# Attention with top-32 masks and two expert layers: one more pipeline step, and for 20 tiles the mask is applied on TensorE

## The chip, the cores and the metric

The kernel runs on one core of a Trainium2 chip. The metric is the device time of one execution in microseconds (us). The engines are TensorE (PE, its weight loads PEld), VectorE (DVE), ScalarE (ACT), GpSimd (POOL) and SyncE (SP), which issues DMAs. Each runs its own queue in order.

## The reference

```python
# q, k, v: (4, 8, 576, 64); top_k = 32
scores = scale * q @ k.T                       # per batch and head, 576 x 576
kth = np.partition(scores, -32)[..., -32:-31]  # 32nd largest of each row
scores = np.where(scores >= kth, scores, -1e9)
attn = softmax(scores); x = attn @ v           # (2304 tokens, 512)
h = x @ w_in                                   # 512 -> 2048
x = (h * clip(h + 3, 0, 6) / 6) @ w_out        # 2048 -> 512
# then: each token goes to one of 8 experts (argmax of x @ w_gate):
out = gate_w * (relu(x @ w1[e]) @ w2[e])       # 512 -> 1024 -> 512
```

## The kernel before

**Tiles.** Attention runs over 144 tiles, each 128 query rows of one head against 576 keys. For a tile t, PE makes the scores (`qk`, in fp32r with the queries split in a high and a low part), ACT copies them out of PSUM (`sevac`, line 300 by way of `copy`), DVE takes the largest values of eight pieces of 72 columns (line 660) and from these the 24 largest (lines 666, 671). The 24th largest, a little lowered, is the value u (`top_c`). The 32nd largest is then found among the scores at or below u: `z` holds the scores with all above u removed, line 731 takes its eight largest, `act_sign` counts on ACT how many scores are above u, and `match` (line 735) picks the one with the right rank as threshold `tall`. `act_exp` makes exp(score - max) on ACT, and `mask` (line 739, DVE, 128x576) sets to zero what is below the threshold. `trans` transposes the masked tile on PE in chunks of 128 columns into the PSUM tile `ptps`, `tevac` copies it out on ACT, `pv` multiplies it with the values, `xevac` divides by the sum, `xt` transposes into the x buffers of the first expert layer.

**The first 20 tiles (`ZPE`).** Their z isn't made on DVE: POOL makes `zw`, -2^100 where the score is above u and 0 elsewhere, in bf16 (`z_pe`, line 703), and PE adds it to a second computation of the scores in the PSUM tile `yps2` (`qk(t, zw)`, line 630). That PSUM tile is used by the first expert layer from about tile 22 on, so later tiles make z on DVE (line 696).

**The layer.** Blocks of 256 tokens are 16 tiles of attention. When all tiles of a block are through `xt`, 16 steps of the first expert layer (`moe_step`: `l1`, line 863; `epi_a`, 869; `epi_b`, 875; `epi_c`; `l2`, line 894) run for it, one for each tile step. Its weights come in 64 bits and are converted on the way, 32 pieces in some 34 tile steps (`conv64`: ACT lines 328, 333; DVE lines 329, 336, 339; POOL lines 298, 347). After the last attention tile the rest of the layer's steps follow, and then the 8 experts (lines 1263, 1286).

**Order.** One loop over tile steps traces all this; each operation gets a priority, 400 a step plus an offset of its kind (`PRIO`), and a scheduler orders each engine's queue by priority among what is ready in its own model. So work of later steps can stand earlier in a queue.

```python
for t in range(T + 7):
    trans(t - 4); top_c(t - 1); act_exp(t - 1)
    qk(t + LA); pv(t - 5); sevac(t + LA); xevac(t - 5)      # LA = 2
    tevac(t - 4); act_sign(t - 1)
    top_a(t, [moe_step, mask(t - 2), conv_next, ...])       # interleaved
    top_z(t - 1); z_pe(t - 1)
```

Of the kernel before, what the change touches and what calls it, by code (L numbers as in the profile page):

```python
# [26 lines left out]

HUGE = 2.0 ** 100
AGE = 0
KB = 1  # L30
LA = 2
# [26 lines left out]
def attention_two_moe_kernel(  # L58
# [169 lines left out]
    def body(cs, exact, ends=None):  # L228
# [160 lines left out]
        if not exact:  # L389
            identb.append(ap1.tile([P, P], BF16, name="identb"))  # L390
            G.tensor_copy(identb[0], ident)
        NPB, NSB, VB = 3, 3 + LA, 2

# [304 lines left out]
        def z_pe(t):  # L698
            if exact or not 0 <= t < ZPE:
                return  # L700
            pr("zw")
            zw = ap1.tile([P, S], F32, tag="z", bufs=2, name=f"z{t}").bitcast(BF16)[:, 0:S]
            G.tensor_scalar(zw, ts[t]["s"][:, 0:S], ts[t]["u"], -HUGE, op0=ALU.is_gt, op1=ALU.mult)
            qk(t, zw)

# [8 lines left out]
        def act_sign(t):  # L714
            if exact:
                return
            pr("sign")
            d = ts[t]
            jk = ap1.tile([P, S], BF16, tag="jk", bufs=1, name=f"jk{t}")
            d["sg"] = ap1.tile([P, 1], F32, tag="sg", bufs=3, name=f"sg{t}")  # L720
            A.activation(jk, d["s"][:, 0:S], AF.Sign, bias=ts[t]["u"], scale=-1.0, accum_out=d["sg"])  # L721

        def mask(t):
            if not 0 <= t < T:
                return
            d = ts[t]
            if not exact:
                pr("max8")
                z8 = ap1.tile([P, 8], F32, tag="z8", bufs=3, name=f"z8_{t}")
                j8 = ap1.tile([P, 8, 2], F32, tag="j8", bufs=1, name=f"j8_{t}")  # L730
                V.max(z8, d["z"])  # L731
                A.activation(zall[:, t:t + 1], z8[:, 1:2], AF.Sign, bias=ts[t]["u"], scale=-1.0)
                yield
                pr("match")
# [11 lines left out]
            yield  # L746


        def trans(t):
            pr("trans")  # L750
# [3 lines left out]
            for c in range(NFC):  # L754
                PE.transpose(ptps[:, c * P:(c + 1) * P], pb[:, c0 + c * P:c0 + (c + 1) * P], ident)  # L755
            if o == "T" or o[0]:
                PE.transpose(ptps[:, N4:SW], pb[:, N4:SW], ident)  # L757

        def tevac(t):
            pr("tevac")  # L760
            d = ts[t]
            o = tiles[t][1]
            if o == "T" or o[0]:
                d["pt"] = ap1.tile([P, SW], F32, tag="ptb", bufs=PTB, name=f"pt{t}")
                copy(mod(t, TPOOL), d["pt"], ptps[:, 0:SW])
            else:
                d["pt"] = ap1.tile([P, N4], F32, tag="pta", bufs=PTA, name=f"pt{t}")
                copy(mod(t, TPOOL), d["pt"], ptps[:, 0:N4])

# [331 lines left out]
        cacc = 0  # L1101
        for t in range(T + 7):
            pr0[0] = pbase + t * STEP
            loads(t)
            if t == 5:
                load_gates(ts[5]["s"])
            while vloaded[0] < NV and (vloaded[0] < VB or vlast[vloaded[0] - VB] <= t - 6):
                load_v()
            ms = moe_step()
            next(ms, None)  # L1110
            if 0 <= t - 4 < T:
                trans(t - 4)
# [6 lines left out]
            if 0 <= t - 5 < T:  # L1119
                pv(t - 5)  # L1120
            if t + LA < T:
                sevac(t + LA)
            if 0 <= t - 5 < T:
                xevac(t - 5)
            xg = None
            if xtq and (xtq[0][2] < t - 5 or t >= T):
                xg = xt(*xtq.pop(0))
                next(xg)
            if 0 <= t - 4 < T:
                tevac(t - 4)  # L1130
            if xg:
# [10 lines left out]
            cacc += CRATE  # L1142
            others = [ms, mask(t - 2)]
            while cacc >= 16:
# [14 lines left out]
        if not exact:  # L1159
            fl = ap1.tile([P, S], F32, tag="z", bufs=2, name="fl")[:, 0:T]  # L1160
            V.tensor_scalar(fl, zall, 0.0, None, op0=ALU.is_le)
            V.scalar_tensor_tensor(fl, uall, HUGE, fl, op0=ALU.is_ge, op1=ALU.add)
            V.scalar_tensor_tensor(fl, tall, 0.0, fl, op0=ALU.is_le, op1=ALU.add, accum_out=flag[:, 0:1])
        pr0[0] += STEP
# [295 lines left out]
```

## Time and profile before

| what | value |
|---|---|
| median of 3 runs | 1199.18 us (1198.66 to 1202.45) |
| profiled execution | 1204.39 us, span 1202.5 us |
| busy in the span | PE 93%, PEld 83%, DVE 78%, ACT 67%, POOL 38% |
| mean granted clock of TensorE | 0.961 of full |
| chain that ended last | PE 71%, DVE 16%, issue 5%, ACT 4% |

Busy time is the time in which an engine has an instruction at work; a matmul's end is modelled, so PE busy is not PE at its peak. Idle time of an engine that isn't the limit costs nothing. The stages differ: PE is below 80% busy up to about 150 us and above 95% later.

### The profile page before, as it was taken

To read this page: it belongs to the slowest core of one execution; us is meant where nothing else is said; L and a number is where in the kernel's file an instruction comes from. 1 tells how busy PE (TensorE), PEld (TensorE's weight loads), DVE (VectorE), ACT (ScalarE), POOL (GpSimd) and SP (SyncE) were. 2 spreads that over 40 slices of the span, in tenths; PEclk is the share of its full clock that TensorE was granted. 3 is DMA by queue.
4 is the path that set the end of the run, shared out by engine and by line. 5 is a ranking of instruction groups with operands and counts; after the bars stand their busy time and mean duration, and the time that the engine had idled before them with its cause. 6 is when DMAs were issued, how large, how long until landed. Compare 5 with 4: busy or idle time off the path is not lost.

```text
span 1202.5 us, 24061 instructions
## 1 busy us (share of the span) xinstructions
PE 1118.5 (93%) x7414; PEld 1003.8 (83%) x7414; DVE 940.9 (78%) x3853; ACT 807.6 (67%) x2082; POOL 458.5 (38%) x668
## 2 busy tenths in 40 slices
PE   5677688999999999999999999999999899999995
PEld 4566577778999989999988899999888799888885
DVE  5989989999999999998999899999641554545540
ACT  4777877778878788778778788777541353444441
POOL 5877646644332354433342432322344311222110
PEclk9668879999999999999999999999999899999998
DMA  3654456564553555754444554543486555455530
GB/s 76 189 179 142 143 171 221 162 174 125 157 134 113 151 134 142 177 135 135 118 122 126 133 147 125 152 133 110 127 271 163 176 187 179 161 176 185 160 121 31
DMA packets 184123, 179.24 MB, mean 149 GB/s; under 512 B 123629, under 2 KB 148509, under 8 KB 183984
## 3 DMA queue, kind: packets, MB, share of 16 engines
q1 hardware_dynamic: 178960, 167.24, 48.3%
q0 software_dynamic: 3872, 10.08, 2.6%
q8 instruction: 61, 1.00, 0.4%
q14 instruction: 78, 0.64, 0.2%
q10 hardware_dynamic: 1152, 0.28, 0.1%
HBM read 159.53 MB, written 18.61 MB: 148 GB/s over the span
## 4 chain that ended last, share of the span: by engine, by line
PE 71%; DVE 16%; issue 5%; ACT 4%; POOL 2%; DMA 2%; SPq 0%; POOLq 0%; ACTq 0%; DVEq 0%
PE l1ps L863 15%; PE yps L894 13%; PE ptps L789 9%; PE lp L1263 8%; PE ops L1286 8%; PE sps L630 6%; PE ptps L755 4%; DVE cd L660 2%; DVE pbuf L739 2%; DVE z L696 2%; DVE z L731 1%; PE ptps L935 1%; DVE m L666 1%; DVE cw L671 1%; PE misc L474 1%
## 5 line engine op out<-in xcount | busy, mean ns | idle before, releaser
L894 PE MATMUL yps<-wo,gh 128*128 128x512 f32 x544 | 206.7, 418 | 0.1
L298 POOL TENSOR_SCALAR gh<-gf 128x256 fp32r<-128x256 f32 x144 | 72.7, 505 | 345.2 <-PE yps L894 196.0
L660 DVE MAX8 cd<-sbuf 128x8 f32<-128x72 f32 x1152 | 187.9, 218 | 3.4 <-ACT sbuf L300 3.2
L863 PE MATMUL l1ps<-xh,wih 128*128 128x256 f32 x576 | 167.6, 291 | 4.7 <-DVE gf L875 3.1
L863 PE MATMUL l1ps<-xh,wil 128*128 128x256 f32 x576 | 164.0, 285 | 0.0
L863 PE MATMUL l1ps<-xl,wih 128*128 128x256 f32 x576 | 163.9, 285 | 0.0
L789 PE MATMUL ptps<-vn,pt 128*128 128x65 f32 (+1 forms) x1152 | 145.8, 281 | 0.0
L789 PEld LDWEIGHTS ptps<-vn,pt 128*128 128x128 f32 x1152 | 143.0, 201 | 0.0
L739 DVE SCALAR_TENSOR_TENSOR pbuf<-sbuf,tall,pbuf 128x576 f32<-128x576 f32 x144 | 136.8, 950 | 0.1
L883 POOL TENSOR_TENSOR gl<-gf,gh 128x256 fp32r<-128x256 f32 x144 | 125.5, 871 | 11.4
L863 PEld LDWEIGHTS l1ps<-xh,wih 128*128 128x128 f32 x576 | 110.4, 192 | 14.9 <-DVE gf L875 7.6
L1036 DVE TENSOR_TENSOR wl<-raw,wh 128x1024 fp32r<-128x1024 f32 x64 | 78.6, 1236 | 53.7 <-ACT wh L1035 51.6
L721 ACT ACTIVATE jk<-sbuf,uall 128x576 bf16<-128x576 f32 x144 | 111.6, 775 | 4.2 <-DVE j L735 0.9
L863 PEld LDWEIGHTS l1ps<-xl,wih 128*128 128x128 f32 x576 | 110.6, 192 | 4.2
L712 ACT ACTIVATE pbuf<-sbuf,nb 128x576 f32<-128x576 f32 x144 | 111.2, 775 | 4.1 <-PE ptps L757 0.9
L894 PEld LDWEIGHTS yps<-wo,gh 128*128 128x128 f32 x544 | 101.2, 190 | 14.8 <-POOL qh L486 0.3
L300 ACT ACTIVATE sbuf<-sps 128x576 f32<-128x576 f32 x144 | 92.9, 645 | 30.4 <-PE sps L630 16.5
L869 ACT ACTIVATE gf<-l1ps,three 128x256 f32<-128x256 f32 x144 | 67.9, 471 | 66.9 <-PE l1ps L863 55.7
L755 PE MATMUL ptps<-ident,pbuf 128*128 128x128 f32 x576 | 93.9, 286 | 19.7 <-DVE j L735 12.6
L894 PE MATMUL yps<-wo,gl 128*128 128x512 f32 x272 | 110.4, 406 | 0.6 <-POOL gl L883 0.6
L863 PEld LDWEIGHTS l1ps<-xh,wil 128*128 128x128 f32 x576 | 110.6, 192 | 0.1
L630 PE MATMUL sps<-kx,qh 128*128 128x288 f32 (+2 forms) x336 | 96.8, 319 | 14.3 <-ACT sbuf L300 10.5
(259 smaller groups left out, 2974.7 us busy)
## 6 DMA issues: line engine op xcount, KB each, us to landing
wo<-wod SPq DMA_DIRECT2D x144, 512.0 KB, 3.8
raw<-in_moe_w_dram SPq DMA_DIRECT2D x64, 512.0 KB, 4.3
vn<-in_v_dram SPq DMA_DIRECT2D x96, 128.0 KB, 2.7
rawi<-in_moe_w_in_dram SPq DMA_DIRECT2D x16, 512.0 KB, 4.0
rawo<-in_moe_w_out_dram SPq DMA_DIRECT2D x16, 512.0 KB, 4.6
wod<-wc SPq DMA_DIRECT2D x16, 512.0 KB, 5.6
qn<-in_q_dram SPq DMA_DIRECT2D x126, 64.0 KB, 2.5
yd<-y SPq DMA_DIRECT2D x18, 258.0 KB, 5.1
```

The lines of the kernel that those rows point to most:

```text
L630: PE.matmul(d_, a_, b_, start=(i == 0), stop=(i == len(mm) - 1))
L660: V.max(cd[:, c, :], s[:, c * CK:(c + 1) * CK])
L712: A.activation(d["p"], d["s"], AF.Exp, bias=d["nb"], scale=SCALE)
L721: A.activation(jk, d["s"][:, 0:S], AF.Sign, bias=ts[t]["u"], scale=-1.0, accum_out=d["sg"])
L739: V.scalar_tensor_tensor(d["p"], d["s"], tall[:, t:t + 1], d["p"], op0=ALU.is_ge, op1=ALU.mult)
L755: PE.transpose(ptps[:, c * P:(c + 1) * P], pb[:, c0 + c * P:c0 + (c + 1) * P], ident)
L789: PE.matmul(d_, a_, b_, start=(i == 0), stop=(i == len(mm) - 1))
L863: PE.matmul(dst, a[:, c, fs], b_[:, c, :], start=(n == 0), stop=(n == 3 * NCC - 1))
L883: G.tensor_tensor(gl, gf, r_(gh), op=ALU.subtract)
L894: PE.matmul(acc(bk, tt), a[:, tsl], b_, start=(f == 0 and m == 0), stop=(f == NF1 - 1 and m == 2))
L1263: PE.matmul(lp, a[:, c, fs], b_[:, c, 0:w], start=(n == 0), stop=(n == 3 * NCC - 1))
L1286: PE.matmul(ops_[j][0:n], a, b_[:, ns], start=(f == 0 and i == 0), stop=(f == NF2 - 1 and i == len(ms) - 1))
```

## The change

For all tiles the work behind u moves one tile step later: exp from t - 1 to t - 2, the maximum of z and its sign (`second`) and `mask` from t - 2 to t - 3, `trans` and `tevac` from t - 4 to t - 5, `pv` and `xevac` from t - 5 to t - 6; the loop has one step more, the ring of score tiles one buffer more (6), that of sign sums 4 in place of 3. For the first 20 tiles POOL makes max(score - u, 0) in fp32r, and PE multiplies it with -2^100 times the identity (`z_mm`, a step later). In these tiles DVE masks only 64 of 576 columns. For the other 512, ACT makes Relu(threshold - score) (`below`), PE adds that tile, transposed by a product with -2^100 times the identity, to each chunk of the transposed exp, and `tevac` takes a Relu of the sum, which turns what is far below zero into zero. The fp32r identity and three tiles for Relu's result lie in the x buffers of block 1, not in use yet. The y transpose `yt` shares the three buffers of the conversion in place of one of its own.

```diff
-            identb.append(ap1.tile([P, P], BF16, name="identb"))
-            G.tensor_copy(identb[0], ident)
-        NPB, NSB, VB = 3, 3 + LA, 2
+            identb.append(xbuf[1][1][:, 2, 0:P])
+            G.tensor_scalar(identb[0], ident, -HUGE, 0.0, op0=ALU.mult, op1=ALU.add)
+        wmask = [xbuf[1][i][:, c:c + 2, :].rearrange("p c t -> p (c t)") for i, c in ((0, 0), (0, 2), (1, 0))]
+        NPB, NSB, VB = 3, 4 + LA, 2
...
-            zw = ap1.tile([P, S], F32, tag="z", bufs=2, name=f"z{t}").bitcast(BF16)[:, 0:S]
-            G.tensor_scalar(zw, ts[t]["s"][:, 0:S], ts[t]["u"], -HUGE, op0=ALU.is_gt, op1=ALU.mult)
-            qk(t, zw)
+            zw = ap1.tile([P, S], F32R, tag="z", bufs=2, name=f"z{t}")
+            G.tensor_scalar(zw, ts[t]["s"][:, 0:S], ts[t]["u"], 0.0, op0=ALU.subtract, op1=ALU.max)
+            ts[t]["zw"] = zw
+        def z_mm(t):
+            if not exact and 0 <= t < ZPE:
+                qk(t, ts[t]["zw"])
...
+        def second(t):
+            ...
+            d["z8"] = ap1.tile([P, 8], F32, tag="z8", bufs=3, name=f"z8_{t}")
+            V.max(d["z8"], d["z"])
+            A.activation(zall[:, t:t + 1], d["z8"][:, 1:2], AF.Sign, bias=ts[t]["u"], scale=-1.0)
...
             pr("mask")
+            if r_pe(t):                                  # not exact and t < ZPE
+                h = tiles[t][1][0]
+                main, tail = slice(h * TAIL, h * TAIL + N4), slice(0, TAIL) if h else slice(N4, S)
+                d["w"] = wmask[t % 3], d["s"][:, main], tall[:, t:t + 1]
+                V.scalar_tensor_tensor(d["p"][:, tail], d["s"][:, tail], tall[:, t:t + 1], d["p"][:, tail], op0=ALU.is_ge, op1=ALU.mult)
+                yield
+                return
...
+        def below(t):
+            if not 0 <= t < ZPE or exact:
+                return
+            pr("exp")
+            w, s, thr = ts[t]["w"]
+            A.activation(w, s, AF.Relu, bias=thr, scale=-1.0)
...
-                PE.transpose(ptps[:, c * P:(c + 1) * P], pb[:, c0 + c * P:c0 + (c + 1) * P], ident)
+                dst, src = ptps[:, c * P:(c + 1) * P], pb[:, c0 + c * P:c0 + (c + 1) * P]
+                PE.matmul(dst, src, ident, start=True, stop=not r_pe(t), is_transpose=True)
+                if r_pe(t):
+                    PE.matmul(dst, wmask[t % 3][:, c * P:(c + 1) * P], identb[0], start=False, stop=True)
...
-                copy(mod(t, TPOOL), d["pt"], ptps[:, 0:SW])
+                A.activation(d["pt"], ptps[:, 0:SW], AF.Relu if r_pe(t) else AF.Copy)
...
-            yt = (wp[0] if last else m1p).tile([P, NCC, P], F32, tag="yt", bufs=1 + last, name=f"yt{i}")
+            yt = (wp[0] if last else m1p).tile([P, NCC, P], F32, tag="yt" if last else "cvs", bufs=2 if last else 3, name=f"yt{i}")
...
-        for t in range(T + 7):
+        for t in range(T + 8):
...
-            while vloaded[0] < NV and (vloaded[0] < VB or vlast[vloaded[0] - VB] <= t - 6):
+            while vloaded[0] < NV and (vloaded[0] < VB or vlast[vloaded[0] - VB] <= t - 7):
...
-            if 0 <= t - 4 < T:
-                trans(t - 4)
+            if 0 <= t - 5 < T:
+                trans(t - 5)
             if 0 <= t - 1 < T:
                 top_c(t - 1)
-                act_exp(t - 1)
+            if 0 <= t - 2 < T:
+                act_exp(t - 2)
+            second(t - 3)
+            z_mm(t - 2)
+            below(t - 4)
...                                       # pv, xevac: t - 6; tevac: t - 5
-            others = [ms, mask(t - 2)]
+            others = [ms, mask(t - 3)]
```

The flag that asks for the exact second pass now also counts thresholds up to 2^-40 in place of 0.

## Rows read from the trace of the kernel before

**Rows 1.** Windows: us; busy PE, PEld, DVE, ACT, POOL; granted clock; DMA share, GB/s.

```profile
18.30:138.80 120.50, 84.75 (x456) 71.58 (x455) 109.44 (x424) 93.39 (x243) 91.49 (x71) 0.77 0.53 153
144.00:240.00 96.00, 83.09 (x523) 71.63 (x522) 92.37 (x351) 74.48 (x200) 52.17 (x68) 0.91 0.59 185
300.00:860.00 560.00, 553.72 (x4068) 510.77 (x4068) 521.37 (x2442) 444.32 (x1246) 192.15 (x319) 1.00 0.51 136
```

**Rows 2.** The chain from 495 to 530 us: start, us, what.

```profile
495.32 1.43 PE l1ps L863 x12
...
497.73 0.44 PE ptps L755 x4
498.17 1.96 PE ptps L789 x18
500.13 1.45 PE yps L894 x6
```

**Rows 3.** Source lines 339, 863, 869: ns min/median/max, first and last start us.

```profile
L339 DVE SCALAR_TENSOR_TENSOR cvo<-rawo,cvo x16: 670/679/1745, 38.0 to 239.2; 128x512 uint32<-128x512 uint32 x16
...
L863 PE MATMUL l1ps<-xh,wih x24: 274/374/581, 72.4 to 189.6; 128*128 128x256 f32 x24
...
L869 ACT ACTIVATE gf<-l1ps,three x5: 464/467/473, 150.5 to 184.6; 128x256 f32<-128x256 f32 x5
```

**Rows 4.** Source line 703, whole span.

```profile
L703 POOL TENSOR_SCALAR z<-sbuf,uall x20: 2207/2219/3045, 18.3 to 138.8; 128x576 bf16<-128x576 f32 x20
```

**Rows 5.** Waits of ACT and of PE, 18.3 to 138.8 us: us, times, longest.

```profile
ACT kx L452 <- PE misc L449: 6.1, 4, 2.4
...
PE ptps L755 <- DVE j L735: 7.5, 4, 3.7
PE sps L630 <- ACT sbuf L300: 7.4, 7, 1.7
```

**Rows 6.** Line 739 by window and over the span; groups by form, line 1268.

```profile
18.30:138.80 120.50, 19.98 (x18) 0.77 0.53 153
...
L739 DVE SCALAR_TENSOR_TENSOR pbuf<-sbuf,tall,pbuf x144: 792/810/1924, 23.5 to 863.3; 128x576 f32<-128x576 f32 x144
...
L1268 DVE SCALAR_TENSOR_TENSOR hb<-lp,hb 128x64 fp32r<-128x64 f32 x24 | 5.1, 214 | 0.0
```

**Rows 7.** The page's costliest groups: busy us, mean ns, idle before.

```profile
L721 ACT ACTIVATE jk<-sbuf,uall 128x576 bf16<-128x576 f32 x144 | 111.6, 775 | 4.2 <-DVE j L735 0.9
L869 ACT ACTIVATE gf<-l1ps,three 128x256 f32<-128x256 f32 x144 | 67.9, 471 | 66.9 <-PE l1ps L863 55.7
```

**Rows 8.** Timeline near 20 and 139 us, and the window around the latter.

```profile
20.42 0.20 ACT L681 ACTIVATE nb<-m 128x1 f32<-128x1 f32 x1
20.52 0.20 ACT L684 ACTIVATE uall<-m 128x1 f32<-128x1 f32 x1
...
138.65 0.46 PE L630 MATMUL yps<-z,identb 128*128 128x288 bf16 x1
139.15 0.45 PE L630 MATMUL yps<-kx,ql 128*128 128x288 f32 x1
139.39 1.06 PE L755 MATMUL ptps<-ident,pbuf 128*128 128x128 f32 x4
...
138.60:140.45 1.85, 1.85 (x10) 1.79 (x9) 1.85 (x9) 1.50 (x3) 1.75 (x2) 0.50 1.03 373
```

**Rows 9.** Groups by form on POOL.

```profile
L298 POOL TENSOR_SCALAR wc<-cvo 128x512 fp32r<-128x512 f32 x16 | 9.9, 616 | 23.9 <-DVE cvo L339 23.8
```

**Rows 10.** Groups on DVE from 144 to 240 us, and line 336 in that window.

```profile
L739 DVE SCALAR_TENSOR_TENSOR pbuf<-sbuf,tall,pbuf 128x576 f32<-128x576 f32 x14 | 14.9, 1061 | 0.0
...
L731 DVE MAX8 z<-z 128x8 f32<-128x576 f32 x12 | 8.9, 740 | 0.0
...
L875 DVE SCALAR_TENSOR_TENSOR gf<-gf,l1ps 128x256 f32<-128x256 f32 x12 | 4.9, 410 | 1.4 <-ACT gf L869 1.4
...
144.00:240.00 96.00, 9.00 (x13) 0.91 0.59 185
```

More of the change, by code (lines that the diff above doesn't have):

```diff
@@ L28 @@
 HUGE = 2.0 ** 100
+SMALL = 2.0 ** -40
 AGE = 0
@@ L719, in act_sign @@
             jk = ap1.tile([P, S], BF16, tag="jk", bufs=1, name=f"jk{t}")
-            d["sg"] = ap1.tile([P, 1], F32, tag="sg", bufs=3, name=f"sg{t}")
+            d["sg"] = ap1.tile([P, 1], F32, tag="sg", bufs=4, name=f"sg{t}")
             A.activation(jk, d["s"][:, 0:S], AF.Sign, bias=ts[t]["u"], scale=-1.0, accum_out=d["sg"])
+        def second(t):
+            if exact or not 0 <= t < T:
+                return
+            d = ts[t]
+            pr("max8")
+            d["z8"] = ap1.tile([P, 8], F32, tag="z8", bufs=3, name=f"z8_{t}")
+            V.max(d["z8"], d["z"])
+            A.activation(zall[:, t:t + 1], d["z8"][:, 1:2], AF.Sign, bias=ts[t]["u"], scale=-1.0)
         def mask(t):
@@ L727, in mask @@
             if not exact:
-                pr("max8")
-                z8 = ap1.tile([P, 8], F32, tag="z8", bufs=3, name=f"z8_{t}")
+                pr("match")
                 j8 = ap1.tile([P, 8, 2], F32, tag="j8", bufs=1, name=f"j8_{t}")
[L731 to L734, printed above, removed]
+                z8 = d["z8"]
                 V.scalar_tensor_tensor(j8, psum_isum, d["sg"], z8.unsqueeze(2).to_broadcast([P, 8, 2]), op0=ALU.is_equal, op1=ALU.mult,
@@ L746, in mask, with r_pe @@
             yield
+        def r_pe(t):
+            return not exact and t < ZPE
+        def below(t):
+            if not 0 <= t < ZPE or exact:
+                return
+            pr("exp")
+            w, s, thr = ts[t]["w"]
+            A.activation(w, s, AF.Relu, bias=thr, scale=-1.0)
         def trans(t):
@@ L764, in tevac @@
                 d["pt"] = ap1.tile([P, SW], F32, tag="ptb", bufs=PTB, name=f"pt{t}")
-                copy(mod(t, TPOOL), d["pt"], ptps[:, 0:SW])
+                A.activation(d["pt"], ptps[:, 0:SW], AF.Relu if r_pe(t) else AF.Copy)
             else:
                 d["pt"] = ap1.tile([P, N4], F32, tag="pta", bufs=PTA, name=f"pt{t}")
-                copy(mod(t, TPOOL), d["pt"], ptps[:, 0:N4])
+                A.activation(d["pt"], ptps[:, 0:N4], AF.Relu if r_pe(t) else AF.Copy)
         def pv(t):
@@ L1118, in body @@
                 qk(t + LA)
-            if 0 <= t - 5 < T:
-                pv(t - 5)
+            if 0 <= t - 6 < T:
+                pv(t - 6)
             if t + LA < T:
                 sevac(t + LA)
-            if 0 <= t - 5 < T:
-                xevac(t - 5)
+            if 0 <= t - 6 < T:
+                xevac(t - 6)
             xg = None
-            if xtq and (xtq[0][2] < t - 5 or t >= T):
+            if xtq and (xtq[0][2] < t - 6 or t >= T):
                 xg = xt(*xtq.pop(0))
                 next(xg)
-            if 0 <= t - 4 < T:
-                tevac(t - 4)
+            if 0 <= t - 5 < T:
+                tevac(t - 5)
             if xg:
@@ L1162, in body @@
             V.scalar_tensor_tensor(fl, uall, HUGE, fl, op0=ALU.is_ge, op1=ALU.add)
-            V.scalar_tensor_tensor(fl, tall, 0.0, fl, op0=ALU.is_le, op1=ALU.add, accum_out=flag[:, 0:1])
+            V.scalar_tensor_tensor(fl, tall, SMALL, fl, op0=ALU.is_le, op1=ALU.add, accum_out=flag[:, 0:1])
         pr0[0] += STEP
```

## The prediction

> **What bounds the kernel now.** I read the stages first, then the chain, then the groups of single engines. The stage rows [rows 1] show three stretches. From 18.3 to 138.8 us, where the first 20 tiles get their threshold, DVE is busy 109.44 of 120.5 us (90.8%), ACT 93.39 (77.5%), POOL 91.49, PE 84.75 at a mean granted clock of 0.77. From 144 to 240 us DVE is busy 92.37 of 96 (96%) and PE has 13 us free. After 240 us PE is the limit: 98.9% from 300 to 860 us at clock 1.00, and the chain there is PE work placed end to end [rows 2]. So only the stretch up to 240 us can be shortened by taking work from DVE; it ends with the weight conversion, whose last DVE step starts at 239.2 us [rows 3]. Behind it, time is PE work, and what PE has not done by then must be paid.
>
> The pace of the first stretch is read from the POOL operation that exists only for these 20 tiles: first start 18.3, last 138.8 us, so 6.34 us a tile over 19 intervals [rows 4]. The longest waits of ACT and PE there, 6.1, 7.5 and 7.4 us [rows 5], are for three different engines: queues that run in order and hold each other, with DVE the fullest.
>
> **The mask of 20 tiles leaves DVE.** L739 has 18 runs in this stretch, 19.98 us, so 1.11 us each; its shortest run is 0.79 and its longest 1.92 us [rows 6]. What stays is a 64-column product; the nearest row is a 128x64 operation of the same kind, 0.21 us [rows 6]. DVE loses 18 x (1.11 - 0.21) = 16.2 us here: 109.4 becomes 93.2.
>
> **ACT gains a Relu of 512 columns.** A 576-column activation with a per-row bias takes 0.775 us and a 256-column Relu with a bias 0.471 us [rows 7]: 0.95 ns a column, so 0.71 us for 512. Neighbouring activations overlap by 0.1 us (starts 20.42 and 20.52, each 0.20 long) [rows 8], so 0.62 us of occupied time; over 19 intervals 11.8 us, and ACT rises from 93.4 to 105.2 us. ACT becomes the fullest engine. Relu in place of Copy in the evacuation costs nothing: same operation, shape and operands.
>
> A rule speaks against this: the Trainium skill, ScalarE: Activation LUTs, section Rules for kernel authors, sends relu, max and mul to VectorE. By that rule the 0.90 us should stay on DVE; by the rows ACT has more room than DVE, 27.1 us idle against 11.1. By the rule the stretch would be 11.8 us longer, by the rows it gets shorter; which holds hangs on whether ACT's idle time can be used, and that is the rival on the slower side below.
>
> **PE gains 80 products of 128 columns.** None of this form is in the trace. From below, four transposes cost 0.44 us in a full stream [rows 2], 0.11 each; from above, four at a granted clock of 0.50, the lower of its two levels (1.2 GHz), cost 1.06 us including the end of the last [rows 8], 0.26 each. That is 0.44 to 1.06 us a tile. I take 0.7, which is 13 us in the stretch: PE 84.8 becomes 98, still under ACT. Product and transpose one behind the other on one region are a sequence that no row shows; I take no extra for it, within the same two ends. The z product turns from bf16 to fp32r: at the same clock it takes 0.46 us, its fp32r neighbour of 288 columns 0.45 [rows 8]; cover is PE's idle time, and without it at most 0.1 us x 40 = 4 us.
>
> **POOL.** The compare-and-multiply becomes subtract-and-max with an fp32r result. Above: 2.2 us as now [rows 4]; below: 0.62 us, a 512-column POOL operation with fp32r result [rows 9]. POOL isn't the fullest either way (91.5, or 91.5 - 20 x 1.6 = 60 us). A shorter one would leave DVE's slow L739-like operations nearer their minimum, but DVE has then room to spare. I take no time for it. The identity in fp32r and the three scratch tiles in block 1's x buffers cost one POOL write before the first tile, which sits in a wait for data.
>
> **Edits at nothing.** Larger rings (scores, sign sums) and the three-deep y transpose only remove waits. No DMA is added; V loads move one step with the step that frees their buffer. The threshold of the flag is a constant. The added waits are below's on the threshold (behind it in ACT's queue: exp, score evacuation, sign) and the products' on below. Match, mask, transposes and P V all move by the same step, so their distances in the order of priorities stay, and I expect no new PE wait in the full stretch after 300 us.
>
> **One step deeper.** Everything behind the threshold comes one tile later, so the first expert-layer block starts one step later against the tiles. At 240 us PE then has one layer step and the second half of one tile still to do: 1.43 + 1.45 for the two layers, 0.44 for transposes, 0.98 for half of a pair's P V products (1.96) [rows 2], together 4.3 us. In exchange DVE has not done, by the same conversion step, one mask (1.06), one z maximum (0.74) and one L875 (0.41) [rows 10]: 2.2 us. The net is 2.1 us if DVE sets 240 us fully and 4.3 us if not. I take 3.0. The added loop round at the end costs nothing: from 860 us PE is fed by layer steps anyway.
>
> **The sum.** With ACT as limit, the stretch is 105.2 us divided by the share at which the limit engine runs: 90.8% as DVE now in this stretch gives 115.9, 96% as DVE in the next gives 109.6. Between them 112.7, so 7.8 us less than 120.5; minus 3.0 for depth is 4.8 us. The profiled execution took 1204.39 us for a span of 1202.5, the median of the runs is 1199.18; the difference is carried to the median: 1194.4 us. Bounds: 10.9 - 2.1 = 8.8 less, 1190.4; 4.6 - 4.3 = 0.3 less, 1198.9. About 0.3%, 3.6 us, is what a measurement of this kernel tells from no change: 1195.6 to 1202.8.
>
> **Rivals.** (a) *ACT's waits stay.* The Relu sits in ACT's in-order queue and waits for match; the score evacuation behind it is late, PE's next scores with it (7.4 us of that wait are there already [rows 5]). If ACT's idle time (120.5 - 93.4 = 27.1 us) stays, the stretch grows by 11.8, and with depth by 14.8: 1214. It decides from 12.3 us of idle time on (27.1 - 11.8 - 3.0); at 20 us the time is 1207. For it: 6.1 us of ACT's waits are for key preparation on PE (L449) [rows 5], which the change doesn't touch. Against: ACT was not the fullest engine [rows 1], so part of its idle time was want of work that a faster DVE now delivers. (b) *Conversion moves forward.* DVE time freed in the first 20 tiles is used for conversion pieces that now run from 144 to 240 us (13 of 32 [rows 10]), so the whole DVE-bound stretch shortens by the 18 us taken from DVE (20 x 0.90), minus 3: 1184. For it: work is taken ahead of its turn already, the first layer's products start at 72.4 us while the layer's first epilogue comes at 150.5 [rows 3]. ACT would need 93.4 + 74.5 + 11.8 = 180 of about 198 us in the two stretches, 91%. Against: three load buffers, and each piece needs ACT too (L328, L333), now the scarce engine. (c) *The gain is eaten.* The stretch shortens by 3 us or less, as in-order waits between four engines of 80% and more replace DVE, and depth takes it back: 1199.
>
> **Chances.** Forecast case 0.42, of which two thirds below 1195.6; (b) 0.20; (c) 0.15; (a) 0.23. Faster by over 0.3%: 0.28 + 0.20 = 0.48; within: 0.14 + 0.15 = 0.29; slower 0.23. The range takes (b) at its 1184 with one us beyond it and (a) up to 20 us of idle time: 1183 to 1207. Faster and slower cases together hold most of the chance, so the likeliest one's own range is 1190 to 1199.
>
> **What would show it.** L739 in the first 20 tiles near 0.2 us; a Relu of 0.7 us a tile in ACT's queue, without waits for match; pace of the POOL operation 5.9 us a tile in place of 6.34; ACT above 90% and DVE near 83% from 18 to 130 us; the last conversion step near 232 us; PE after 300 us unchanged. Wrong, if ACT stays under 85% there, or if the conversion ends before 225 us, or if the full PE stretch changes by more than 3 us from its new order.

## The result and the profile after

The changed kernel takes 1208.66 us (median of 6 runs, 1206.70 to 1212.04), the kernel before 1201.86 us in the same comparison: ratio 1.0065, 95% interval 1.0049 to 1.0082. It is slower by 6.8 us where the forecast was 4.8 us less (1194.4 us), and its median lies above the range, which ended at 1207. The profiled execution after took 1212.04 us, with a span of 1210.3 us against 1202.5.

Windows of the profile after (columns as in [rows 1]); the first is from the first to the last start of POOL's operation of the first 20 tiles:

```profile
18.00:146.20 128.20, 92.48 (x513) 82.02 (x511) 113.20 (x448) 98.13 (x254) 91.74 (x73) 0.78 0.51 152
144.00:240.00 96.00, 82.28 (x519) 72.06 (x519) 88.37 (x337) 76.25 (x210) 47.12 (x60) 0.88 0.59 183
300.00:860.00 560.00, 554.26 (x4075) 511.87 (x4075) 522.16 (x2450) 446.51 (x1257) 185.84 (x320) 1.00 0.50 135
```

The stretch forecast to fall to 112.7 us grew from 120.5 [rows 1] to 128.2. No engine is full in it: DVE 88%, ACT 77%, PE and POOL 72%. The pace is 6.75 us a tile in place of 6.34. From 144 to 240 us DVE has fallen from 96% to 92% and the granted clock from 0.91 to 0.88. From 300 to 860 us nothing differs by more than 1%, except POOL, which has 6 us less to do.

Source lines of the profile after: ns min/median/max, first and last start us.

```profile
L705 POOL TENSOR_SCALAR z<-sbuf,uall x20: 2203/2210/2889, 18.0 to 146.2; 128x576 fp32r<-128x576 f32 x20
...
L775 ACT ACTIVATE xh<-sbuf,tall x14: 708/722/727, 25.2 to 164.5; 128x512 fp32r<-128x512 f32 x14
...
L754 DVE SCALAR_TENSOR_TENSOR pbuf<-sbuf,tall,pbuf x20: 263/362/1386, 24.1 to 164.5; 128x64 f32<-128x64 f32 x20
...
L786 PE MATMUL ptps<-xl,xh x56: 307/309/455, 38.9 to 172.5; 128*128 128x128 f32 x56
...
L340 DVE SCALAR_TENSOR_TENSOR cvo<-rawo,cvo x16: 667/676/1657, 43.5 to 243.5; 128x512 uint32<-128x512 uint32 x16
...
L900 ACT ACTIVATE gf<-l1ps,three x144: 453/475/524, 172.2 to 935.6; 128x256 f32<-128x256 f32 x144
```

The single costs are near their estimates: the Relu 0.72 us (0.71), POOL's new form 2.21 us as the old one [rows 4]. Of the products, two transposes in a row in the timeline of after, each with its product behind it, at the full clock:

```profile
164.72 0.30 PE L784 MATMUL ptps<-ident,pbuf 128*128 128x128 f32 x1
164.78 0.31 PE L786 MATMUL ptps<-xl,xh 128*128 128x128 f32 x1
164.92 0.30 PE L784 MATMUL ptps<-ident,pbuf 128*128 128x128 f32 x1
```

The pair takes 0.20 us from start to start, a transpose alone 0.11 [rows 2], so a product adds some 0.09 us, just under the lower of the prediction's two bounds. The 64-column mask takes 0.36 us in the middle and up to 1.39, not 0.21. What came out otherwise is the order of the whole: the last conversion step starts at 243.5 us in place of 239.2, the first layer epilogue at 172.2 in place of 150.5 [rows 3].

Waits of ACT and of PE in the profile after, 18 to 160 us (us, times, longest):

```profile
ACT xh L775 <- DVE j L746: 5.2, 6, 1.5
ACT xl L775 <- DVE j L746: 4.8, 4, 3.4
...
PE ptps L784 <- DVE j L746: 12.5, 10, 4.4
...
PE yps L632 <- POOL z L705: 6.2, 6, 2.1
```

The Relu waits for match (line 746 here), 10.0 us in 10 waits; PE's transposes wait for match 12.5 us.

**Three measures of a run.** (1) The ratio to before, with its interval. (2) How late the 41st and the last of the 144 first-layer steps start, counted by the products of line 863 (894 after) in the profile: before, 400.4 and 926.0 us. It is one execution: the y-ring kernel below has the time of before and comes out 4.5 us early, so 5 us of lateness proves little. (3) Means over the timed runs, less those of before on the same chip: the span, its low-clock share (span times one minus the granted clock of the run), and the rest, which is nothing but the difference of the two.

The low-clock share is bookkeeping and not a price: it counts a low clock also while TensorE is idle. Over 73 runs before has a span of 1200.8 us and a share of 44.1. Between these runs, 1 us more of share goes with 0.5 us more of span (correlation 0.80; 0.3 to 0.8 us on single chips). So a change of the share can't be read as time won or lost, and a "rest" that grows while the span stays need not be work that was paid.

| kernel | ratio (95%) | 41st step | last step | span | low clock | rest |
|---|---|---|---|---|---|---|
| after (against all runs of before) | 1.0065 (1.0049–1.0082) | +8.3 | +7.9 | +6.5 | +0.2 | +6.3 |
| e1 after, mask on DVE | 1.0137 (1.0113–1.0162) | +14.0 | +21.0 | +17.4 | +12.7 | +4.7 |
| e2 after, old depth | 1.0253 (1.0220–1.0286) | +18.5 | +22.4 | +29.3 | +18.8 | +10.5 |
| e4 before, mask left out | * | -1.1 | -0.5 | | | |
| e3 after, no Relu, no products | * | +2.7 | +4.0 | | | |
| f2 after, products alone | * | -0.5 | +4.6 | | | |
| f1 after, Relu alone | * | +11.0 | +10.0 | | | |
| f3 before, new z | 1.0013 (0.9991–1.0034) | -0.6 | -0.3 | +1.6 | -2.5 | +4.1 |
| h3 before, y ring | 1.0010 (0.9992–1.0028) | -5.1 | -4.5 | +0.1 | -1.2 | +1.2 |
| f4 before, all rings | 1.0075 (1.0058–1.0092) | +2.4 | +3.4 | +7.9 | -0.8 | +8.8 |
| h1 after, Relu later | 1.0143 (1.0107–1.0178) | +4.1 | +10.0 | +15.1 | +8.8 | +6.3 |
| h2 after, Relu without match | 1.0153 (1.0127–1.0179) | +5.4 | +10.9 | +17.4 | +18.1 | -0.6 |
| h4 after, Relu on DVE | 1.0080 (1.0052–1.0107) | +1.1 | +7.3 | +8.8 | -1.4 | +10.3 |
| i1 after, products twice | 1.0037 (1.0015–1.0058) | -4.2 | -1.8 | +5.5 | -2.7 | +8.2 |
| i2 after, conversion later | 1.0039 (1.0012–1.0066) | +3.3 | +4.7 | +5.1 | +2.6 | +2.5 |
| i3 depth and zero products | 1.0102 (1.0069–1.0136) | +9.2 | +10.9 | +13.5 | 0.0 | +13.5 |
| j1 before, zero products | 0.9997 (0.9981–1.0012) | -3.1 | -1.6 | -0.4 | -9.7 | +9.2 |
| j2 before, three times those | 1.0168 (1.0145–1.0191) | +17.1 | +17.1 | +21.1 | +10.7 | +10.4 |

\* With the mask left out the routing changes and an overflow phase of 134 to 137 us follows the common program, at 1.2 GHz; only the steps are compared. h2's mask is another one too, so its routing and the work behind its last step differ; it is read at the steps.

### The profile page after: what moved, and what is told of

Its sections match the earlier page's. It is cut to its first block, busy times and chain, and to the rows that moved or that the text cites. A ratio compares the mean times of both kernels' runs of the same rounds, so it can differ in the third digit from the quotient of the medians.

```text
span 1210.3 us, 24311 instructions
## 1 busy us (share of the span) xinstructions
PE 1126.2 (93%) x7494; PEld 1015.9 (84%) x7494; DVE 941.0 (78%) x3853; ACT 814.3 (67%) x2102; POOL 447.9 (37%) x668
## 4 chain that ended last, share of the span: by engine, by line
PE 72%; DVE 13%; issue 5%; DMA 4%; ACT 3%; POOL 2%; SPq 0%; POOLq 0%; ACTq 0%; DVEq 0%
PE l1ps L894 15%; PE yps L925 14%; PE ptps L820 10%; PE lp L1298 8%; PE ops L1321 8%; PE sps L632 5%; PE ptps L784 5%; DVE cd L662 2%; DVE z L735 1%; PE ptps L966 1%; DVE pbuf L757 1%; DMA qn<-in_q_dram 1%; DVE z L698 1%; PE misc L476 1%; PE sps L925 1%
## 5 line engine op out<-in xcount | busy, mean ns | idle before, releaser
L299 POOL TENSOR_SCALAR gh<-gf 128x256 fp32r<-128x256 f32 x144 | 68.4, 475 | 373.1 <-PE yps L925 202.1
L820 PE MATMUL ptps<-vn,pt 128*128 128x65 f32 (+1 forms) x1152 | 143.2, 278 | 0.0
L820 PEld LDWEIGHTS ptps<-vn,pt 128*128 128x128 f32 x1152 | 140.3, 198 | 0.0
L784 PE MATMUL ptps<-ident,pbuf 128*128 128x128 f32 x576 | 100.5, 289 | 17.5 <-DVE j L746 16.7
L757 DVE SCALAR_TENSOR_TENSOR pbuf<-sbuf,tall,pbuf 128x576 f32<-128x576 f32 x124 | 112.6, 908 | 0.1
L698 DVE SCALAR_TENSOR_TENSOR z<-sbuf,uall 128x576 f32<-128x576 f32 x124 | 109.3, 881 | 0.2 <-ACT uall L686 0.2
```

The costliest lines, as they stand in the source:

```text
L698: V.scalar_tensor_tensor(d["z"], s, d["u"], s, op0=ALU.is_le, op1=ALU.mult)
L784: PE.matmul(dst, src, ident, start=True, stop=not r_pe(t), is_transpose=True)
L820: PE.matmul(d_, a_, b_, start=(i == 0), stop=(i == len(mm) - 1))
```

## Experiments

The first four runs set three theories against each other: D, the extra step costs and the mask's move gives nothing; M, the mask's move costs; C, conversion pieces pulled ahead cost.

**e1, the depth without the mask's move.** The larger rings and the new z stay as in after.

```diff
 def r_pe(t):
-    return not exact and t < ZPE
+    return False
```

> The kernel after with the full 576-column mask back on DVE for all tiles: no Relu(threshold - score), no products, Copy evacuation. What stays of the change is the step of depth, the fp32r z of POOL and the rings. Theory D (the step of depth costs, the move of the mask gives nothing): the expert layer starts about one tile step later as after (172 us against 150.5), so 1206 to 1210 us, like after. Theory M (the move of the mask costs, depth is about free): 1199 to 1203 us, like before, and the first layer epilogue comes near 155 us. Theory C (DVE time freed by the move is taken by conversion pieces pulled ahead, which delay the tiles): without freed time the conversion pieces start where they did before, 1199 to 1204 us.

1220.98 us: ratio 1.0137, slower than the whole change and outside all three ranges. M falls: the move is no pure loss. In the deeper order it gives back half of what depth, rings and new z cost together. The low-clock share is 12.7 us larger than before's.

**e2, the mask's move without the depth**, every step back at its old place; the larger rings and the new z stay here too.

```diff
-for t in range(T + 8):
+for t in range(T + 7):
...
-    trans(t - 5)
+    trans(t - 4)
...
-    below(t - 4)
+    below(t - 3)
...
-    others = [ms, mask(t - 3)]
+    others = [ms, mask(t - 2)]
```

> The kernel after with every step of the loop where it was before (second half of a tile one step earlier): the mask of the first 20 tiles still goes by Relu(threshold - score) on ScalarE and products on TensorE. Theory D: without the extra step the move of the mask shows what it is worth alone, no loss: 1197 to 1203 us. Theory M: ACT's Relu and the transposes wait for match, nearer to it by a step than in after: 1208 to 1214 us, at least as slow as after. Theory C: the DVE time is freed here too, so the conversion pieces move ahead as in after and the time is 1205 to 1209 us.

1232.39 us, ratio 1.0253: the slowest of the three, so D falls as well. Both halves, each with the rings and the new z, cost more than the two together. Waits of PE and POOL, 18 to 160 us:

```profile
PE yps L632 <- POOL z L705: 22.3, 11, 3.4
...
POOL z L705 <- ACT uall L686: 20.2, 10, 4.0
```

PE stands 22.3 us for POOL's z (1.4 before, 6.2 after), and POOL 20.2 us for ACT's u (9.3 us before, 13.9 after). A likely reading, not tested by itself: without the step of depth the z product has no time to be late, so when ACT is late, POOL is late and PE idle.

**e4, DVE's relief alone, at the old depth.**

```diff
+if not exact and t < ZPE:
+    V.scalar_tensor_tensor(d["p"][:, tail], d["s"][:, tail], tall[:, t:t + 1], d["p"][:, tail], op0=ALU.is_ge, op1=ALU.mult)
+    yield
+    return
 V.scalar_tensor_tensor(d["p"], d["s"], tall[:, t:t + 1], d["p"], op0=ALU.is_ge, op1=ALU.mult)
```

> The kernel before with only the 64-column tail of the mask done in the first 20 tiles; it leaves out the mask of the other 512 columns there. It is the most that taking the mask from DVE can give at the old depth, as nothing takes its place. By the step of the prediction that DVE sets the stretch: 16 to 18 us of DVE time gone, the time 1184 to 1192 us. Theory D and theory M as rivals of that step: DVE is not alone the limit, POOL's 2.2 us operation and the in-order waits hold the pace at 6.3 us a tile, 1196 to 1202 us. Theory C: the freed time goes to conversion pieces pulled ahead, pace as before or slower, 1198 to 1206 us.

The window of this kernel over the first stretch of [rows 1]:

```profile
18.00:138.80 120.80, 86.41 (x466) 72.81 (x466) 101.46 (x429) 89.42 (x241) 90.16 (x71) 0.76 0.54 154
```

Its source line 703, the pace (columns as in [rows 4]):

```profile
L703 POOL TENSOR_SCALAR z<-sbuf,uall x20: 2207/2210/2768, 18.0 to 138.6; 128x576 bf16<-128x576 f32 x20
```

DVE's two longest waits in it, 18 to 160 us:

```profile
DVE rs L808 <- PE ptps L795: 10.6, 7, 3.4
DVE z L731 <- PE yps L630: 5.9, 3, 2.9
```

This run decides against the forecast. Nothing takes the mask's place, DVE's load in the stretch falls from 109.4 to 101.5 us, and the pace is the same: the 20th z starts at 138.6 against 138.8 us. DVE waits for PE instead. The last layer step is 0.5 us early.

**e3, the change without Relu and products.**

```diff
 def below(t):
...
-    A.activation(w, s, AF.Relu, bias=thr, scale=-1.0)
+    return
...
-    if r_pe(t):
-        PE.matmul(dst, wmask[t % 3][:, c * P:(c + 1) * P], identb[0], start=False, stop=True)
```

> The kernel after without Relu(threshold - score) and without the 80 products; it leaves out the mask of 512 of 576 columns in the first 20 tiles. The depth and DVE's relief stay. Theory D: depth is what costs, so 1205 to 1209 us still, at most the 0.7 us a tile of the Relu come back in part. Theory M: the price was the Relu, the products and their waits; it falls to 1194 to 1201 us. Theory C: the conversion pieces stay pulled ahead, the loss stays: 1205 to 1209 us.

Against e4, depth, rings and new z make the last step 4.5 us later, the 41st 3.8. The full mask on DVE in the same order (e1) makes it 17 us later still. At the old depth the mask's price was 0.5 us. The start of the 20th z shows the same; source line 705 of e1:

```profile
L705 POOL TENSOR_SCALAR z<-sbuf,uall x20: 2202/2274/3219, 18.0 to 145.1; 128x576 fp32r<-128x576 f32 x20
```

The same of e3:

```profile
L705 POOL TENSOR_SCALAR z<-sbuf,uall x20: 2199/2211/2762, 18.0 to 135.7; 128x576 fp32r<-128x576 f32 x20
```

So in the deeper order the full mask on DVE does go with a slower pace, which it did not at the old depth.

**f1 and f2, Relu and products one at a time.** f1 is e3 with the Relu line back; f2 keeps the products, reading a tile of zeros, and leaves out the Relu:

```diff
-    A.activation(w, s, AF.Relu, bias=thr, scale=-1.0)
+    return
...
-    PE.matmul(dst, wmask[t % 3][:, c * P:(c + 1) * P], identb[0], start=False, stop=True)
+    PE.matmul(dst, zero, identb[0], start=False, stop=True)
```

> The kernel after with Relu(threshold - score) still done by ScalarE but without the 80 products, so the mask of 512 of 576 columns in the first 20 tiles is left out; as the routing changes with it, an overflow phase of some 134 us follows at the end, and the comparison is made at the 41st first-layer step (L863 before; it starts at 400.4 us before, 8.3 us later after, 2.7 us later without Relu and products, 1.1 us earlier in the kernel before with that mask left out). Theory ACT (the Relu in ACT's in-order queue, waiting for match, is what costs): 7 to 9 us later, like after. Theory PE (the products are PE time that is not regained): 2 to 4 us later, as without both.

> The kernel after with the 80 products reading one constant tile of zeros, and no Relu(threshold - score); the mask of 512 of 576 columns in the first 20 tiles is left out again, with the overflow phase at the end. Read at the 41st first-layer step. Theory PE: 7 to 9 us later than before, like after. Theory ACT: 2 to 4 us later. If neither run reaches 7 us, the two add up, or the chain from match over Relu to product is the cost.

The first product of the 41st first-layer step in the timeline of f1 (start us, us, what):

```profile
411.46 0.28 PE L892 MATMUL l1ps<-xh,wih 128*128 128x256 f32 x1
```

The same of f2:

```profile
399.91 0.28 PE L896 MATMUL l1ps<-xh,wih 128*128 128x256 f32 x1
```

And of after:

```profile
408.71 0.28 PE L894 MATMUL l1ps<-xh,wih 128*128 128x256 f32 x1
```

With the Relu 11.0 and 8.3 us late, without it 2.7 (e3) and -0.5: the kernels with the Relu are 8.3 and 8.8 us later there, and the products add nothing. Theory ACT fits these four. By the last step the gap is 6.0 (f1 to e3) and 3.3 (after to f2), since f2 and e3 lose time in between (last section). Each is one execution of another order, and i1 below warns: it has the same Relu on ACT, and its 41st step comes 4.2 us early.

**f3 and f4, two edits that the prediction priced at nothing**, each alone in the kernel before.

```diff
-G.tensor_scalar(zw, ts[t]["s"][:, 0:S], ts[t]["u"], -HUGE, op0=ALU.is_gt, op1=ALU.mult)
+G.tensor_scalar(zw, ts[t]["s"][:, 0:S], ts[t]["u"], 0.0, op0=ALU.subtract, op1=ALU.max)
```

> The kernel before with POOL's z in the form of the change alone (subtract and max to fp32r, product with -2^100 times the identity), at its old place. Theory Z (the new form of z comes later or its product is placed earlier, and PE waits for it, as the 22 us of PE's waits for POOL's z in the kernel with the mask moved at the old depth hint): 1208 to 1222 us and PE's waits for L703 above 10 us between 18 and 160 us (1.4 before). Otherwise, as the prediction has it: no change, 1197 to 1205 us.

```diff
-NPB, NSB, VB = 3, 3 + LA, 2
+NPB, NSB, VB = 3, 4 + LA, 2
...
-tag="sg", bufs=3
+tag="sg", bufs=4
...
-tag="yt", bufs=1 + last
+tag="yt" if last else "cvs", bufs=2 if last else 3
```

> The kernel before with only the rings of the change: one more score buffer, one more sign sum, y transposes in a ring of three. The prediction costs this at nothing: 1197 to 1205 us. If it moves the time by more than 5 us, the order that the planner writes for the first 20 tiles is so sensitive that differences of that size between the other runs can't be put down to single operations.

The new z is free. The rings are not: 1.0075, four runs within 0.8 us. By the condition that the expectation set, differences of this size between the other runs can't be put down to single operations. The window of f4 from 200 to 250 us (columns as in [rows 1]):

```profile
200.00:250.00 50.00, 43.60 (x276) 37.06 (x274) 46.60 (x177) 35.49 (x99) 30.62 (x46) 0.93 0.55 171
```

The same window with the y ring alone (h3, the third of the three edits):

```profile
200.00:250.00 50.00, 46.26 (x323) 39.88 (x321) 49.24 (x198) 37.75 (x108) 30.52 (x48) 1.00 0.59 173
```

With the longer score ring PE, DVE and ACT all have less to do between 200 and 250 us, and the clock falls to 0.93; up to 140 us that kernel was 3 us ahead of before (its 20th z starts at 135.5). That the front of the tiles has run ahead can't be the whole reason: the 20th z of h3 starts at 134.9, and h3 loses nothing.

> The kernel before with one thing of the change: the transposed y tiles share the ring of three buffers of the weight conversion, in place of a buffer of their own. All three rings together gave 1.0075. Theory Y (the shared ring ties gate tiles and conversion pieces together, and that is what the rings cost): 1205 to 1210 us. Otherwise the score ring or the sign sums did it: 1197 to 1203 us.

1.0010: the y ring is free. By elimination the score ring with the sign sums costs; these two were not run without the y ring.

**h1, h2 and h4, why the Relu costs.** h1 changes its priority, h2 its threshold, h4 its engine:

```diff
-pr("exp")
+pr("tevac")
```

```diff
-d["w"] = wmask[t % 3], d["s"][:, main], tall[:, t:t + 1]
+d["w"] = wmask[t % 3], d["s"][:, main], d["u"]
```

```diff
-A.activation(w, s, AF.Relu, bias=thr, scale=-1.0)
+V.tensor_scalar(wmask[t % 3], d["s"][:, main], tall[:, t:t + 1], 0.0, op0=ALU.subtract, op1=ALU.min)
```

> The kernel after with Relu(threshold - score) given the priority of ScalarE's transpose evacuation (450 in place of -295), so that the planner puts it later in ACT's queue; nothing else differs. Theory Wait (the Relu stands in ACT's queue ahead of work that is ready and waits there for match, 10 us in 10 waits between 18 and 160 us): those waits go, the 41st first-layer step comes 0 to 4 us later than before in place of 8.3, and the time is 1199 to 1205 us. Theory Load (0.71 us a tile more on ACT is the cost, wherever it stands): 6 to 9 us later, 1206 to 1211 us. If the transposes' products then wait for the Relu instead, the loss stays and PE's waits for it show in the waits for the transposes.

> The kernel after with the Relu taken against the upper bound u (known two steps earlier) in place of the threshold, so it can't wait for match; the mask of the first 20 tiles is then another one, the routing changes, and the comparison is made at the 41st first-layer step. Same load on ACT, PE and DVE. Theory Wait: 0 to 4 us later than before. Theory Load: 6 to 9 us later, as after.

> The kernel after with min(score - threshold, 0) on DVE right behind match in place of the Relu on ScalarE (products with +2^100 times the identity; same result). ACT gets nothing more, DVE keeps 20 operations of 512 columns of 0.5 to 0.8 us (the nearest row, a 512-column one-input operation of the conversion, takes 0.50 to 0.63 us). Without the Relu and the mask, with the products alone, the 41st first-layer step came 0.5 us earlier than before. Theory ACT: DVE's operation costs less than ACT's 8.3 us, so 0 to 4 us later, 1199 to 1204 us. Rival: DVE's time counts as much at this depth as the 11 us between the full mask on DVE and none; half of the mask's time gives 5 to 6 us later, 1204 to 1208 us.

None is faster than after. In h1 the waits for match (18 to 160 us) are down to one line,

```profile
ACT xl L775 <- DVE j L746: 3.5, 2, 2.8
```

from 10.0 us; the 41st step comes 4.2 us earlier than after, and the whole takes 9 us more; its low-clock share is 8.8 us above before's, after's 0.2. h2 can't wait for match at all, and its 41st step, 5.4 us late, lies between the two theories. Theory Wait is not borne out, Theory Load neither: on DVE the operation (0.48 us in the middle for the larger group of 14, up to 2.3) leaves ACT as it was, and the time is 1.0080.

**i1, i2, i3.** The products doubled; the conversion's priority a step later; and e1 with products of zeros:

```diff
-PE.matmul(dst, wmask[t % 3][:, c * P:(c + 1) * P], identb[0], start=False, stop=True)
+PE.matmul(dst, wmask[t % 3][:, c * P:(c + 1) * P], identb[0], start=False, stop=False)
+PE.matmul(dst, wmask[t % 3][:, c * P:(c + 1) * P], identb[0], start=False, stop=True)
```

```diff
-mask=55, conv=295,
+mask=55, conv=695,
```

```diff
 PE.matmul(dst, src, ident, start=True, stop=not zp, is_transpose=True)
+if zp:
+    PE.matmul(dst, zero, identb[0], start=False, stop=True)
```

> The kernel after with each of the 80 products issued twice (the result is the same, as the Relu of the evacuation makes zeros of it either way). Theory Work (PE work in the first 20 tiles is not hidden and comes on top of the end): another 8 us or so of PE work, 1213 to 1218 us. Theory Hidden (the products lie in PE's idle time, as the prediction had it): 1206 to 1210 us, as after.

> The kernel after with the priority of the weight conversion one tile step later (695 in place of 295), so that its pieces are not pulled ahead of the tiles. Theory C (the pieces pulled ahead wait for their loads in DVE's queue and delay the tiles): 1199 to 1204 us. Rival: the pieces only fill time that is free, and later ones push the end of the conversion and the first layer back: 1209 to 1220 us. No change: 1206 to 1210 us.

> The kernel of the depth alone (full mask on DVE, no Relu; 1221 us, of which 58 go to the low clock) with 80 products of a tile of zeros added after the transposes; the result is the same. Theory Fill (the products keep PE active and so its clock granted, and that is what makes the whole change faster than its depth alone): 1207 to 1216 us, with 44 to 50 us lost to the clock. Theory Relief (DVE's relief is what gives the depth's loss back): 1221 to 1230 us, as the products' work is added to the 1221.

The window of the whole early stretch, of after:

```profile
18.00:200.00 182.00, 137.09 (x796) 121.35 (x794) 163.58 (x648) 146.64 (x382) 118.16 (x102) 0.80 0.54 166
```

Of i1, with the products doubled:

```profile
18.00:200.00 182.00, 145.81 (x935) 130.51 (x933) 167.85 (x679) 150.90 (x395) 125.74 (x112) 0.88 0.57 172
```

Of e1:

```profile
18.00:200.00 182.00, 133.89 (x687) 118.36 (x685) 163.72 (x615) 131.54 (x342) 113.06 (x97) 0.75 0.50 153
```

Of i3, e1 with products of zeros:

```profile
18.00:200.00 182.00, 131.90 (x780) 116.67 (x779) 166.82 (x631) 134.74 (x350) 115.37 (x100) 0.81 0.53 159
```

Doubled products are not slower than after (1.0037 against 1.0065, overlapping intervals), so Theory Work falls in this order. The clock reads 0.88 against 0.80 in these two executions; over the timed runs the low-clock share is 2.9 us smaller. Products of zeros take e1's share from 12.7 us above before's to none, and the span falls by 3.9 us, from 1.0137 to 1.0102 with overlapping intervals: Fill is right about the clock, and a gain of time is not clear of the noise.

i2 came out at 1208.38 us, in its range for no change; C had 1199 to 1204. Its ratio, 1.0039 against 1.0065, has an overlapping interval, so that the pieces pulled ahead cost anything is not shown.

> The kernel after with the five score buffers of before in place of six. Theory Ring (one more score buffer lets the first half of the tiles run ahead of the second, the 6 to 8 us that the rings cost at the old depth): 1199 to 1204 us. Rival: at the new depth a score tile lives a step longer, so the sixth buffer is only what keeps the slack, and without it the scores wait for the Relu: 1210 to 1225 us.

i4 tells nothing: it computes something else (1295.45 us), most likely since with five buffers the Relu reads a score tile that a later one has overwritten.

**j1 and j2, filler in the kernel before**, as in i3, with one and with three products (of zeros with zeros) behind each transpose.

> The kernel before with 80 products of a tile of zeros behind the transposes of the first 20 tiles; same result, nothing else changed. Theory Fill (PE work there keeps the granted clock up and lies in idle time): 1195 to 1202 us, and less than 43 us lost to the clock. Theory Work (PE work adds to the end in an order that is not deeper): 1205 to 1210 us.

> The same with three products of zeros for each transpose, 240 in all, about 25 us of PE work at the full clock. Theory Fill: 1195 to 1204 us, with under 36 us lost to the clock. Theory Work: 1215 to 1230 us.

Windows of before, j1 and j2 over 18 to 200 us:

```profile
18.00:200.00 182.00, 136.24 (x753) 117.03 (x753) 167.43 (x649) 139.08 (x360) 121.44 (x105) 0.79 0.54 165
...
18.00:200.00 182.00, 139.89 (x849) 120.42 (x848) 172.60 (x664) 141.60 (x368) 124.62 (x108) 0.85 0.55 170
...
18.00:200.00 182.00, 148.82 (x855) 133.40 (x854) 153.09 (x589) 124.71 (x323) 111.82 (x90) 0.76 0.50 150
```

One product: 1203.29 us, ratio 0.9997, between the ranges of the two theories; the low-clock share is 9.7 us smaller. Three: 1223.83 us, ratio 1.0168, inside the range of Theory Work; the share is 10.7 us larger. So 80 products cost nothing that can be measured at the old depth, and 240 cost 21 us. Whether the 80 simply lie in PE's idle time, or cost time that the higher clock gives back, is not shown: the span stays the same either way. No version tried beats the kernel before.

## Why the prediction was wrong, step by step

**The sum failed at the step "with ACT as limit, the stretch is 105.2 us divided by the share at which the limit engine runs".** It took DVE's 90.8% for the limit of the pace and forecast 7.8 us less with the limit moved to ACT. e4 shows that 90.8% is no limit: with the mask gone and nothing in its place, the pace does not move. [rows 5] had said so: the longest waits name three engines, none above 7.5 us. So had the chain of the kernel before, from 18 to 140 us, by source line:

```profile
by line: issue 8.9%; DVE cd L660 8.5%; DVE pbuf L739 6.6%; PE yps L630 6.2%; PE sps L630 5.2%; DVE cvi L329 4.0%; DVE z L731 3.8%; PE ptps L789 3.8%; DVE cvo L336 3.8%; DVE m L666 3.2%; DVE cvo L339 3.1%; DVE cvi L336 3.0%; DMA qn<-in_q_dra
```

The mask has 6.6% of this chain, 8 us of 122, and no line has more than 9%. Load over share did not hold here, where four in-order queues are all 70 to 91% busy. The prediction's own sign of error came as well: ACT is 76% busy from 18 to 130 us, where less than 85% meant wrong.

The Trainium skill's rule that the prediction weighed (ScalarE: Activation LUTs, section Rules for kernel authors) sends relu to VectorE. On the operation itself the trace agrees, 0.48 us on DVE against 0.72 on ACT; the time of the kernel is the same within the intervals (1.0080 and 1.0065).

**The pace was not the time either.** The prediction read the gain from the first stretch. Two variants of after come close to the pace that it forecast, 5.9 us a tile. Source line 707 of h4:

```profile
L707 POOL TENSOR_SCALAR z<-sbuf,uall x20: 2202/2215/2731, 18.0 to 132.8; 128x576 fp32r<-128x576 f32 x20
```

Source line 705 of i1:

```profile
L705 POOL TENSOR_SCALAR z<-sbuf,uall x20: 2202/2212/2891, 18.0 to 134.0; 128x576 fp32r<-128x576 f32 x20
```

That is 6.0 and 6.1 us a tile. Their last conversion steps start at 236.4 and 231.1 us (239.2 before, 232 forecast), and both are slower than before, 1.0080 and 1.0037. So a shorter first stretch would not have been enough.

**Mask on DVE:** 16.2 us of load were to go; in e4 8 went. The 64-column operation has a mean of 0.45 us where 0.21 was forecast, and about 4 us of other work moved into the stretch. Worth at the old depth 0.5 us.

**Depth, 3.0 us (2.1 to 4.3), and larger rings, nothing:** together 4.5 us at the last step (e3 less e4). That this lies near the depth term is luck as far as the runs show, since the term priced the rings at nothing and alone, without depth, they cost 0.75%. "Only remove waits" failed as a reason. How the 4.5 us divide is open. The term also held only for the lighter DVE: with the full mask, depth and rings cost 17 to 21 us (e1).

**Relu, priced inside the sum:** duration right; its kernels are 3.3 to 6.0 us later at the last step. It resembles rival (a) in outcome: ACT's idle time stayed (128.2 - 98.1 = 30.1 us, 27.1 before), and at over 20 us of it the rival gave 1207 or more. Its reason, the wait for match, is not borne out by h1 and h2. In the first stretch the traces speak for the Relu on ACT as a cause: with it the 20th z starts at 146.2 (after), 150.4 (f1), 144.6 (h1) and 142.2 us (h2), without it at 135.7 (e3), 134.4 (f2) and 132.8 (h4). But i1 has it, with the products doubled, and its 20th z starts at 134.0. That the Relu is the cause of these microseconds is argued, not shown. A rival stands beside it: the larger rings alone cost 1.0075 (1.0058 to 1.0092) at the old depth, as much as the whole loss of 1.0065 (1.0049 to 1.0082). i4, which was to take the score buffer out of after, computed something else, so no run separates the two.

**Products, 0.7 us a tile under cover of PE's idle time:** 80 products cost no time in i1, i3 and j1, as forecast. The granted clock, which the prediction left out of this term, moved with them: up in j1, down with three times as many in j2.

**z, y ring, PE after 300 us:** right (f3, h3, windows).

Put together at the last layer step, along e4, e3, f2 and after: mask gone -0.5, depth and rings +4.5, products +0.6, Relu +3.3. These differences add up to after's 7.9 us by construction, whatever their cause. Along f1 the last two are Relu +6.0 and products -2.1. Each figure is one execution's and carries some 5 us of its own, so the division is an indication and no measurement. Rival (b), conversion pieces pulled ahead, did happen (the 16th of the 32 last conversion steps starts 10.9 us sooner than before) and gave nothing.

**What stays open:** what sets the 6.3 us a tile at the old depth, since taking load from DVE doesn't change it; why doubled products go with a quicker pace (i1); why the full mask on DVE costs so much more at the new depth; why the score ring costs; and whether the loss of after is the Relu's or the rings'.

## What to carry to other kernels

Before taking load off the busiest engine, leave the work out altogether in one run: if the pace stays, there is little to buy, whatever takes its place. Do it in the order that the change will have, too: here the mask was worth 0.5 us in the old order and 17 us in the new one. A ring that "only removes waits" is an edit of the order and has to be timed alone. Where the granted clock is below 1 in a stretch, neither the work added there nor the clock that moves with it is a price; time the kernel with that work alone.

## What the runs showed of the hardware

With 80 small products added to the kernel before (j1) the low-clock share is 35.9 us, the mean of 12 runs, against 45.6 us of 17 runs of before on the same chip, in the same time. With 240 (j2) it is 56.2 us. So added PE work raised the mean granted clock once and lowered it once.

The Trainium skill (TensorE: Matmul & The Clock Gate, section What's actually happening) says that the gate is set by how busy PE has been recently. In the windows from 18 to 200 us above, j1 agrees with that, 139.9 us busy at a clock of 0.85 against 136.2 us at 0.79; j2, 148.8 us busy at 0.76, does not show it, and busy time also grows when the clock is low.

Near 420 us PE waits once for a q load in the deeper kernels. PE's wait in h4, 405 to 440 us:

```profile
PE misc L478 <- DMA qn<-in_q_dram: 2.7, 1, 2.7
```

The windows around it:

```profile
420.00:425.00 5.00, 2.49 (x18) 2.43 (x19) 2.29 (x11) 1.57 (x6) 1.89 (x3) 0.91 0.66 170
425.00:430.00 5.00, 5.00 (x19) 4.42 (x19) 3.64 (x20) 2.02 (x7) 1.79 (x4) 0.50 0.02 4
430.00:435.00 5.00, 5.00 (x35) 4.73 (x34) 2.44 (x6) 3.39 (x9) 2.30 (x4) 0.91 0.35 108
```

The same wait in after, and the window with it:

```profile
PE misc L476 <- DMA qn<-in_q_dram: 1.2, 1, 1.2
...
425.00:430.00 5.00, 3.79 (x31) 3.38 (x30) 3.66 (x16) 3.03 (x8) 1.40 (x4) 1.00 0.86 169
```

In h4, PE runs at half its clock (1.2 GHz) for some 7 us behind its 2.7 us of standing still (the shares of the three windows), and the layer steps are 4 us later behind it than ahead of it. In after, behind 1.2 us, the clock stays at 2.4 GHz. The length of the wait alone does not decide it. The wait of e3, and the window after it:

```profile
PE misc L476 <- DMA qn<-in_q_dram: 1.8, 1, 1.8
...
425.00:430.00 5.00, 5.00 (x33) 4.74 (x33) 4.01 (x22) 2.26 (x7) 2.55 (x4) 0.84 0.13 28
```

The wait of i3, with the window that holds most of it and the next:

```profile
PE misc L479 <- DMA qn<-in_q_dram: 2.6, 1, 2.6
...
425.00:430.00 5.00, 2.84 (x21) 2.48 (x20) 3.69 (x19) 2.65 (x7) 1.14 (x2) 1.00 1.22 133
430.00:435.00 5.00, 4.56 (x34) 4.31 (x35) 3.64 (x19) 2.87 (x8) 3.21 (x5) 1.00 0.27 84
```

e3 falls to the lower clock for a while behind 1.8 us, i3 stays at 2.4 GHz behind 2.6 us. f2, h1, h2 and e1 show the same fall as h4, behind 2.3 to 2.5 us; for f2, h1 and h2 it is most of what makes their last step later than their 41st, for e1 about 4 of 7 us. So one late load in the PE-bound stretch went with about 4 us, as much as the whole depth term.
